# Turning finished rows on TensorE as float32r and as float32 inside the last layer, and adding the scaled difference to the output

## The chip, the cores and the metric

The kernel runs on one core of a Trainium2 chip. The metric is the device time of one execution in microseconds. The engines are named as in the profile: PE (TensorE matmul; PEld its weight loads), DVE (VectorE), ACT (ScalarE), POOL (GpSimd) and SP (SyncE, which here only issues transfers).

## What is computed

Causal attention with a decay bias (4 batches, 8 heads, 576 positions, head size 64), then two feed-forward layers over 2304 tokens with 512 features and 2048 hidden ones:

```python
scores = scale * np.matmul(q, k.transpose(0, 1, 3, 2))
...
attn = attn / (np.sum(attn, axis=-1, keepdims=True) + 1e-09)
x = np.matmul(attn, v)            # to (2304, 512)
h = x @ w_in;  x = np.maximum(0.01 * h, h) @ w_out
h = x @ w2_in; out = (np.maximum(h, 0.0) + np.log1p(np.exp(-np.abs(h)))) @ w2_out
```

All in float32. The kernel gets the precision from float32r matmuls by splitting each operand into a rounded high part and a low part, so that one product is three matmuls (high by high, high by low, low by high).

## The kernel before

Three stages follow one another: attention (to about 237 us), the first layer (to about 565) and the second layer (to the end). The change lies in the second layer alone.

The second layer splits the hidden features into eight blocks of 256 (`NJ = 8`) and four blocks of 512 token rows into two pairs (`PAIRS`; `sb` 0 and 1), beside a remainder of 256 rows (`Plain`). One `Quad` handles one pair and one hidden block: 16 quads, `sb` 0 first. A quad computes its 2 by 2 blocks of hidden values with seven products instead of eight: `X Y K Z X K Z` is the order of the PSUM banks to which the products 1 to 7 go, each of six matmuls. Products 5 to 7 accumulate into banks X, K and Z a second time. Between them, banks are added to each other: `first` (line 1028) copies bank X to an SBUF tile `u` on ACT after product 1, and five `join`s (line 1032) on DVE add `u` and the banks, the last of them into Z. So product 5 may write X only after `first` has read it, and product 6 K only after the second join.

Each of the four blocks of hidden values then passes through a `Unit`, a chain of nine steps: magnitude, exponential, logarithm and total on ACT, value and rest on DVE, correct on POOL, high on ACT (the rounded part) and low on POOL (the remainder). After the seven products of quad n come the eight output groups of quad n-1 (`outputs`, `emit_out`, line 1065): six matmuls each into a bank from `tail_bank`, which deals out three PSUM banks in turn, and one DVE instruction that adds the bank to `acc` (line 1086; a copy for the first hidden block). `acc` holds the output in SBUF with 128 token rows to a slot; after the last hidden block of a pair its rows are written to `out`.

The order is written out by hand. `on(t, fn)` puts a call into a list with a time in units of one product or output group; the list is sorted by that time at the end and the calls are made in this order. Each engine takes its instructions in the order in which they are made, and so does each engine's queue of transfers; nothing reorders them. A unit that begins at b has its steps at b plus 0, 0.45, 0.9, 1.35, 1.4, 1.85, 2.4, 4.1 and 5.5. In quad n, which begins at `starts[n]`, the products stand at +0 to +6, `first` at +1.05, the joins at +2.05, +3.05, +4.05, +6.05 and +7.05, the units at +5.1 and 2.6 further each, and the output groups of the quad before at +7 to +14. From the tenth quad on the next one begins at +15. `fetch` brings weights for coming quads through SP: those of the outputs of the next quad at +1, and at +9 the eight tiles of the products of the quad after it, each of which waits until its buffer is free.

The last row block pair's quads have index 8 to 15, so `starts[12]` is the fifth of the second pair. The rows 0 to 127 that the change uses were finished with quad 7.

Of the kernel before, what the change touches and what calls it, by code (L numbers as in the profile page):

```python
# [10 lines left out]
F32 = mybir.dt.float32  # L11
I32 = mybir.dt.int32
U32 = mybir.dt.uint32
F32R = mybir.dt.float32r
AF = mybir.ActivationFunctionType
ALU = mybir.AluOpType
PSUM = bass.MemoryType.PSUM

P = 128
# [12 lines left out]
def attn_moe_moe(ctx, tc, q, k, v, s, w1i, w1o, w2i, w2o, out):  # L32
    nc = tc.nc
# [17 lines left out]
    def pool(name, bufs=1, **kw):  # L51
        return tc.tile_pool(name=name, bufs=bufs, **kw)
# [28 lines left out]
    def move(dst, src, queue=nc.sync):  # L81
        queue.dma_start(dst.bitcast(F32), src.bitcast(F32))
# [457 lines left out]
    class Fill:  # L540
# [32 lines left out]
        def bank(self, nm):  # L573

            tag, bufs = ("m", 1) if not self.free else self.free.pop(0)
            if self.free is not None:
                self.free.append((tag, bufs))
            return self.ps.tile([P, 512], F32, tag=tag, name=nm, bufs=bufs)
# [88 lines left out]
    acc = ctx.enter_context(pool("accpool")).tile([P, KD, NT], F32, tag="acc", name="acc")  # L667
    stages = [ExitStack(), ExitStack()]
    enter = lambda stage, nm, **kw: stages[stage].enter_context(pool(nm, **kw))
# [200 lines left out]
    for g in range(1, NG):  # L870
        a = begin[g - 1]
        own = (1, 4, 7, 11, 15, 18, 16, 19) if g > 1 else (None,) * 4 + (3, 6, 4, 7)
        for j, n in enumerate(own):
            if n is not None:
                w = (0, g * G + j // 2, "io"[j % 2])
# [16 lines left out]
    k = begin[NG - 1, chunks[1]] + G + LAG  # L892
# [14 lines left out]
    for n, (g, c, f) in enumerate(steps):  # L907
        N = c[1]
        cols = slice(c[0], c[0] + N)
        ps = bank("ps_h")  # L910
# [21 lines left out]
    def on(t, fn, *args):  # L932
        events.append((t, len(events), fn, args))
# [3 lines left out]
    def tail_bank(nm):  # L937
        tag, bufs = next(tails)
        return psA.tile([P, 512], F32, tag=tag, name=nm, bufs=bufs)
# [185 lines left out]
    t = 0  # L1125
    starts = []
# [26 lines left out]
    for kp in range(2):  # L1153
# [5 lines left out]
        for n, nm in enumerate(("B11", "T3", "T2", "B21", "T4"), 1):  # L1159
# [3 lines left out]
            else:  # L1163
                on(b + 3, x_high, 1, nm, kp)
                on(b + 5, x_low, 1, nm, kp, nc.gpsimd)

    for t, _, fn, args in sorted(events, key=lambda x: x[:2]):
        fn(*args)
    stages[1].close()
# [47 lines left out]
```

## Time and profile before

| | us |
|---|---|
| median of 3 runs | 951.94 |
| lowest, highest | 951.5, 951.96 |
| the profiled execution | 951.81 |
| its span, first to last instruction | 950.0 |

| engine | busy us | share |
|---|---|---|
| PE | 941.3 | 99% |
| DVE | 668.0 | 70% |
| ACT | 575.8 | 61% |
| POOL | 564.3 | 59% |

The profile is one execution, with times in us from its first instruction. Busy shares are means over stages; a wait or a duration of one place is read from the timeline of that place. Matmuls are pipelined: a matmul of 512 columns is shown with 0.39 us, while the next starts 0.23 us after it, so a stream of matmuls is paid by the distance of its starts.

### The profile page before, as it was taken

The page shows a single profiled execution, that of the slowest core. Times are in us where ns is not written, and L with a number is a line of the kernel's source. Part 1 is how long each engine was busy: PE and PEld are TensorE (multiplying, and loading weights), DVE is VectorE, ACT ScalarE, POOL GpSimd, SP SyncE. Part 2 cuts the span into 40 slices and gives each one's busy share as a digit, 9 for nine tenths or more (in the row PEclk, how much of TensorE's full clock was granted, in tenths as well). Part 3 has the DMA queues.
Part 4 walks back from the last instruction along what each step waited for, and adds up shares of the span by engine and source line. Part 5 has one row for each costly group of instructions (what it writes and reads, how often), then busy time and mean ns, then how long its engine had stood idle before and what let it go on. Part 6 is the DMA issues. An engine that isn't in the chain of part 4 may idle for free.

```text
span 950.0 us, 15346 instructions
## 1 busy us (share of the span) xinstructions
PE 941.3 (99%) x5173; PEld 767.3 (81%) x5173; DVE 668.0 (70%) x1294; ACT 575.8 (61%) x1185; POOL 564.3 (59%) x548
## 2 busy tenths in 40 slices
PE   9999999999999999999999999999999999999998
PEld 6666767777998888888888888888888888888887
DVE  8888656554479798778998745665666666766666
ACT  6888677665566564546555446666656765565563
POOL 7778556444367676657666534755654664555443
PEclk9999999999999999999999999999999999999999
DMA  7453434331665654546476244341415248445402
GB/s 248 148 164 127 144 111 134 119 106 37 215 239 180 229 190 139 173 166 213 132 269 217 102 151 159 115 136 66 153 65 177 89 150 314 135 136 175 134 0 90
DMA packets 79251, 143.61 MB, mean 151 GB/s; under 512 B 7626, under 2 KB 24906, under 8 KB 79172
## 3 DMA queue, kind: packets, MB, share of 16 engines
q1 hardware_dynamic: 78740, 141.87, 44.9%
q8 instruction: 41, 0.67, 0.3%
q10 hardware_dynamic: 432, 0.75, 0.3%
q14 instruction: 38, 0.31, 0.1%
HBM read 109.33 MB, written 33.25 MB: 150 GB/s over the span
## 4 chain that ended last, share of the span: by engine, by line
PE 93%; DVE 3%; POOL 1%; ACT 1%; issue 1%; DMA 0%; SPq 0%; DVEq 0%; POOLq 0%; ACTq 0%
PE ps_h L145 20%; PE ps_out L1078 20%; PE ps_out L854 17%; PE ps_h L1023 16%; PE pt_s L316 4%; PE pt_t L377 3%; PE ps_o L635 3%; PE pt_v L409 3%; PE ps_h L1105 2%; PE pt_s L409 1%; PE pt_t L372 1%; PE pt_s L302 1%; DVE sc L337 1%; POOL sc L360 0%; ACT sc L349 0%
## 5 line engine op out<-in xcount | busy, mean ns | idle before, releaser
L974 POOL TENSOR_TENSOR l<-l,e 128x512 f32<-128x512 f32 x72 | 93.5, 1298 | 161.8 <-DVE e L971 147.5
L151 POOL TENSOR_TENSOR gl<-gf,gh 128x512 fp32r<-128x512 f32 (+2 forms) x68 | 88.7, 1305 | 111.7 <-ACT gh L150 78.5
L360 POOL TENSOR_SCALAR sc<-sc,st 128x512 f32<-128x512 f32 (+4 forms) x160 | 88.4, 563 | 79.2 <-DVE st L356 61.3
L145 PE MATMUL ps_h<-xh,wih 128*128 128x512 f32 (+2 forms) x320 | 119.9, 375 | 0.0
L145 PE MATMUL ps_h<-xh,wil 128*128 128x512 f32 (+2 forms) x320 | 118.1, 369 | 0.0
L145 PE MATMUL ps_h<-xl,wih 128*128 128x512 f32 (+2 forms) x320 | 117.9, 368 | 0.0
L1086 DVE TENSOR_TENSOR acc<-ps_out,acc 128x512 f32<-128x512 f32 (+1 forms) x127 | 86.8, 685 | 42.5 <-PE ps_out L1078 40.0
L1078 PE MATMUL ps_out<-woh,gh 128*128 128x512 f32 x290 | 112.5, 388 | 0.8 <-DVE acc L1086 0.8
L1078 PE MATMUL ps_out<-wol,gh 128*128 128x512 f32 x290 | 112.4, 388 | 0.0
L349 ACT ACTIVATE sc<-sc,st 128x512 f32<-128x512 f32 (+2 forms) x144 | 83.4, 582 | 34.5 <-DVE st L337 28.7
L854 PE MATMUL ps_out<-gh,woh 128*128 128x512 f32 (+2 forms) x272 | 99.2, 365 | 0.3 <-DVE acc L861 0.3
L854 PE MATMUL ps_out<-gh,wol 128*128 128x512 f32 (+2 forms) x272 | 99.1, 364 | 0.0
L854 PE MATMUL ps_out<-gl,woh 128*128 128x512 f32 (+2 forms) x272 | 99.0, 364 | 0.0
L834 ACT ACTIVATE gf<-ps_h 128x512 f32<-128x512 f32 (+2 forms) x68 | 37.1, 546 | 101.4 <-PE ps_h L145 92.7
L984 POOL TENSOR_TENSOR gl<-l,gh 128x512 fp32r<-128x512 f32 x72 | 93.6, 1308 | 3.0 <-ACT gh L980 3.0
L1078 PE MATMUL ps_out<-woh,gl 128*128 128x512 f32 x290 | 88.9, 388 | 0.0
L980 ACT ACTIVATE gh<-l 128x512 fp32r<-128x512 f32 x72 | 45.4, 630 | 66.0 <-POOL l L974 66.0
L1023 PE MATMUL ps_h<-xh,wih 128*128 128x512 f32 x208 | 81.0, 389 | 0.0
L1023 PE MATMUL ps_h<-xl,wih 128*128 128x512 f32 x208 | 81.0, 389 | 0.0
L1023 PE MATMUL ps_h<-xh,wil 128*128 128x512 f32 x208 | 80.9, 389 | 0.0
L337 DVE CUSTOM_DVE_ANT_0 sc<-pt_s,mask 128x512 f32<-128x512 f32 (+3 forms) x129 | 59.2, 483 | 16.2 <-PE pt_t L377 15.4
L145 PEld LDWEIGHTS ps_h<-xh,wil 128*128 128x128 f32 x320 | 60.2, 188 | 9.6
(168 smaller groups left out, 2369.7 us busy)
## 6 DMA issues: line engine op xcount, KB each, us to landing
w2d<-stg SPq DMA_DIRECT2D x88, 256.0 KB
rawi<-in_moe_w_in SPq DMA_DIRECT2D x32, 512.0 KB
rawo<-in_moe_w_out SPq DMA_DIRECT2D x32, 512.0 KB
wih<-w2d SPq DMA_DIRECT2D x64, 256.0 KB
wil<-w2d SPq DMA_DIRECT2D x64, 256.0 KB
woh<-w2d SPq DMA_DIRECT2D x32, 256.0 KB
wol<-w2d SPq DMA_DIRECT2D x32, 256.0 KB
K<-in_k SPq DMA_DIRECT2D x15, 432.0 KB
```

Source lines behind the costliest of these rows:

```text
L145: nc.tensor.matmul(ps, a, b, start=kk == 0 and n == 0, stop=kk == KD - 1 and n == 2)
L151: nc.gpsimd.tensor_tensor(gl, gf, gh.bitcast(F32), op=ALU.subtract)
L337: nc.vector.tensor_tensor_reduce(out=self.sc[:, j, c], in0=self.ps[j][:, c], in1=m, scale=-scale, scalar=low, op0=ALU.add, op1=ALU.min, ac ...
L349: nc.scalar.activation(x, x, AF.Exp, scale=-1.0, bias=self.stat(0, e + self.last), accum_out=self.stat(1, e))
L360: nc.gpsimd.tensor_scalar(x, x, self.stat(2, e), 1.0, op0=ALU.mult, op1=ALU.mult)
L854: nc.tensor.matmul(ps, a, b, start=f == 0 and m == 0, stop=f == G - 1 and m == 2)
L974: nc.gpsimd.tensor_tensor(self.l, self.l, self.e, op=ALU.subtract)
L980: nc.scalar.activation(self.gh, self.l, AF.Copy)
L984: nc.gpsimd.tensor_tensor(self.gl, self.l, self.gh.bitcast(F32), op=ALU.subtract)
L1023: nc.tensor.matmul(self.ps[name], x, y, start=n < 4 and kp == 0 and m == 0, stop=kp == 1 and m == 2, skip_group_check=n >= 4,)
L1078: nc.tensor.matmul(u, a, v, start=m == 0, stop=m == len(ops) - 1)
L1086: nc.vector.tensor_tensor(d[..., w], o[..., w], d[..., w], op=ALU.add)
```

## The change

New tiles `ident`, `ident_r`, `copy` and `apart` are placed behind all others in the last layer's memory. In quad 12 the following is added: an identity matrix on POOL and its rounded copy on ACT; a transfer on SP of 384 columns of finished rows 0 to 127 from `acc` to a float32r tile, bit for bit; 12 transposes on PE of this copy as float32r and 12 of `acc` as float32 (three blocks of 128x128, four times over), into two banks from `tail_bank`; on DVE a copy of the first bank to SBUF, the difference of the second to it, and the difference times 1e12 added to `acc`; and a transfer of the 384 columns to `out`.

```diff
+    def prepare_look():
+        make_identity(nc, ident)
+        nc.scalar.activation(ident_r, ident, AF.Copy)
+        move(copy, acc[:, 0, :384])
+
+    def turn(nm, x, y):
+        ps = tail_bank("ps_x")
+        ps = seen[nm] = ps.bitcast(F32R) if nm == "r" else ps
+        for k in range(4):
+            for c in range(3):
+                w = slice(c * P, (c + 1) * P)
+                nc.tensor.transpose(ps[:, w], x[:, w], y)
+
+    def compare():
+        d, o = apart, acc[:, 0, :384]
+        nc.vector.tensor_copy(d, seen["r"].bitcast(F32)[:, :384])
+        nc.vector.tensor_tensor(d, seen["f"][:, :384], d, op=ALU.subtract)
+        nc.vector.scalar_tensor_tensor(o, d, 1.0e12, o, op0=ALU.mult, op1=ALU.add)
+        nc.sync.dma_start(out[:P, :384], o)
+
+    t = starts[12]
+    on(t + 1, prepare_look)
+    on(t + 6.9, turn, "r", copy, ident_r)
+    on(t + 6.95, turn, "f", acc[:, 0, :512], ident)
+    on(t + 7.4, compare)
```

`make_identity` is two POOL instructions: a memset of the 128x128 tile to zero and an affine select that puts 1.0 on the diagonal. `nc.tensor.transpose` is one weight load of the data and one matmul that streams the identity. `move` is a transfer on SP.

## Rows read from the trace of the kernel before

**Rows 1.** The page: busy time by engine, and granted TensorE clock in 40 slices, tenths.
```profile
PE 941.3 (99%) x5173; PEld 767.3 (81%) x5173; DVE 668.0 (70%) x1294; ACT 575.8 (61%) x1185; POOL 564.3 (59%) x548
...
PEclk9999999999999999999999999999999999999999
```
**Rows 2.** Chain that ended last, 850 to 950: start, length, engine, line, instructions.
```profile
853.88 9.52 PE ps_h L1023 x42
863.39 10.88 PE ps_out L1078 x48
```
**Rows 3.** Busy time (instructions) of one quad: PE, PEld, DVE, ACT, POOL; clock; DMA.
```profile
853.70:874.10 20.40, 20.40 (x91) 16.89 (x90) 13.67 (x21) 12.26 (x21) 10.20 (x9) 1.00 0.49 155
```
**Rows 4.** Timeline of POOL in this quad: start, duration, instruction, idle time before.
```profile
855.94 1.29 POOL L974 TENSOR_TENSOR l<-l,e 128x512 f32<-128x512 f32 x1 [0.83 <-DVE e L971]
857.19 2.55 POOL L984 TENSOR_TENSOR gl<-l,gh 128x512 fp32r<-128x512 f32 x2
```
**Rows 5.** Timeline of ACT in this quad.
```profile
855.27 0.60 ACT L1030 ACTIVATE u<-ps_h 128x512 f32<-128x512 f32 x1 [0.76 <-PE ps_h L1023]
857.27 0.63 ACT L980 ACTIVATE gh<-l 128x512 fp32r<-128x512 f32 x1 [1.40 <-POOL l L974]
```
**Rows 6.** Timeline of PE: first product, fifth product, first output group.
```profile
853.71 0.39 PE L1023 MATMUL ps_h<-xh,wih 128*128 128x512 f32 x1
...
859.15 0.62 PE L1023 MATMUL ps_h<-xp,wih 128*128 128x512 f32 x2
...
863.23 0.39 PE L1078 MATMUL ps_out<-woh,gh 128*128 128x512 f32 x1
```
**Rows 7.** Timeline of POOL at the start of the kernel.
```profile
3.16 0.30 POOL L437 TENSOR_SCALAR_AFFINE_SELECT mask<-mask 128x128 f32<-128x128 f32 x1
...
4.11 0.20 POOL masks.py:197 MEMSET ident<- 128x128 f32 x1
4.38 1.28 POOL masks.py:199 TENSOR_SCALAR_AFFINE_SELECT ident<-ident 128x128 f32<-128x128 f32 x1
```
**Rows 8.** Timeline of DVE at the start of the kernel.
```profile
4.15 1.42 DVE L213 TENSOR_TENSOR_SCAN PB<-V,st,sc 128x576 f32<-128x576 f32 x1 [0.21 <-ACT sc L212]
```
**Rows 9.** Groups of ACT by form: busy us, mean ns of one, idle before.
```profile
L150 ACT ACTIVATE gh<-gf 128x512 fp32r<-128x512 f32 x48 | 29.9, 624 | 0.0
...
L150 ACT ACTIVATE gh<-gf 128x256 fp32r<-128x256 f32 x12 | 4.9, 407 | 0.1
```
**Rows 10.** Timeline of SP's transfer issues in this quad.
```profile
855.00 0.42 SPq L82 DMA_DIRECT2D wol<-w2d  x1
859.12 0.32 SPq L82 DMA_DIRECT2D wih<-w2d  x1
```
**Rows 11.** Busy time in one slice, columns as in rows 3; last is GB/s.
```profile
857.00:858.00 1.00, 1.00 (x6) 0.83 (x5) 0.40 (x2) 0.63 (x1) 1.00 (x2) 1.00 0.92 344
```
**Rows 12.** Timeline of PE in the attention stage, around six transposes.
```profile
112.55 0.82 PE L377 MATMUL pt_t<-ident,sc 128*128 128x128 f32 x6
113.12 0.47 PE L635 MATMUL ps_o<-gh,woh 128*128 128x512 f32 x1
113.43 0.39 PE L635 MATMUL ps_o<-gl,woh 128*128 128x512 f32 x1
```
**Rows 13.** Timeline of PE, two matmuls of 256 columns in a stream.
```profile
764.37 0.28 PE L1105 MATMUL ps_h<-xh,wil 128*128 128x256 f32 x1
764.49 0.28 PE L1105 MATMUL ps_h<-xh,wih 128*128 128x256 f32 x1
```
**Rows 14.** Instructions that write the transposes' tile: ns min/median/max, first and last start.
```profile
L377 PE MATMUL pt_t<-ident,sc x320: 270/273/330, 12.6 to 235.6; 128*128 128x128 f32 x160
```
**Rows 15.** Timeline of DVE in this quad: first accumulation of an output group, last join.
```profile
864.79 0.69 DVE L1086 TENSOR_TENSOR acc<-ps_out,acc 128x512 f32<-128x512 f32 x1 [0.76 <-PE ps_out L1078]
865.40 0.69 DVE L1040 TENSOR_TENSOR ps_h<-ps_h,u 128x512 f32<-128x512 f32 x1
```
**Rows 16.** Groups of DVE by form.
```profile
L391 DVE COPY PB<-pt_t 128x384 f32<-128x384 f32 x32 | 17.7, 554 | 32.8 <-PE pt_t L377 32.5
```

More of the change, by code (lines that the diff above doesn't have):

```diff
@@ L1165, in attn_moe_moe @@
                 on(b + 5, x_low, 1, nm, kp, nc.gpsimd)
+    look = enter(1, "look", side="right")
+    ident = look.tile([P, P], F32, tag="id", name="id")
+    ident_r = look.tile([P, P], F32R, tag="idr", name="idr")
+    copy = look.tile([P, 384], F32R, tag="cp", name="cp")
+    apart = look.tile([P, 384], F32, tag="ap", name="ap")
+    seen = {}
+    def prepare_look():
[20 more added lines that the diff above has]
+    on(t + 7.4, compare)
     for t, _, fn, args in sorted(events, key=lambda x: x[:2]):
```

## The prediction

> **What bounds the kernel now.** I read the page first: PE is busy 941.3 of 950.0 us, at a granted clock of nine tenths or more in every slice [rows 1]. A share over the whole span says nothing of one stage, so next I read the chain that ended last, over its last 100 us. It holds only PE, 42 product matmuls and 48 output matmuls in turn, up to the kernel's last output groups [rows 2]. The new work goes into the fifth quad of the second pair of row blocks (event time `starts[12]`). Its seven products start at 853.71 and end at 863.23, so six matmuls take 1.36 us and the eight output groups behind them, of the quad before, end at 874.1 [rows 6]. Over this stretch PE is busy 20.40 of 20.40 us at clock 1.00, while DVE has 13.67, ACT 12.26 and POOL 10.20 [rows 3]. So here each microsecond that PE is given or kept waiting comes out at the end, and nothing in PE's queue can give it back. The other engines matter only where PE waits for them.
>
> **Order first.** In this stage each engine's queue is the event list sorted by time. The trace bears this out: POOL does the fourth unit's subtraction (+0.3) at 855.94, then the third unit's low part (+0.8) and the fourth's (+3.4) as a pair from 857.19 [rows 4]. So I can place each new instruction. Positions below are event times relative to `starts[12]`.
>
> **Step 1: the identity (+1), a wait for PE.** POOL gets a memset and an affine select, ACT a rounding copy `ident_r` that needs both, and on ACT this copy stands ahead of `first` (+1.05), the copy of bank X into `u`. Behind the waiting ACT instruction are thus queued `first`, the fourth unit's high part and the next magnitude. `first` is the one that counts: the fifth product accumulates into bank X, so it may not start before `first` has read it. In the trace `first` runs from 855.27 to 855.87 and the fifth product starts at 859.15 [rows 5, 6], a cover of 3.3 us. When can POOL serve? The identity falls between the two low parts of the pair, which takes 2.55 us [rows 4], so at 858.46. The memset takes 0.20, with 0.27 to the next start. The select has two prices: 0.30 for the mask of the same size, 1.28 for the first identity [rows 7]. The second ran beside a DVE scan of 1.42 us and ended 0.09 us behind it [rows 8]. In the new place DVE has nothing to do, since its next three joins wait for `u`. I take 0.30 and keep 1.28 for the range. [...]
>
> POOL is then done at 858.46 + 0.27 + 0.30 = 859.03. For ACT's copy of 128 columns, 407 ns at 256 and 624 at 512 columns [rows 9] go down to about 0.30. With 0.04 for the handover (855.94 + 1.29 on POOL to ACT's 857.27) it ends at 859.37, `first` (0.60) at 859.97, and PE goes on at about 860.05: 0.9 us late [rows 4 to 6]. With the 1.28 us select it is 1.9; without any wait 0. DVE's joins follow `u` at 0.6 us each [rows 15], so the second is over at 861.3, as the fifth product ends at 861.4: no second wait, but no room either. POOL's last low part slips behind ACT's late high part to about 862; it is needed by the second half of the outputs, behind 868. That costs nothing, and would if `first` came over 4 us later still.
>
> **Step 2: the copy of the rows (+1).** One transfer of 196 KB from SBUF to SBUF on SP, behind four weight loads of 262 KB, the last issued at 855.00 [rows 10]. Its source has been ready long since. The trace has no such transfer; at the 344 GB/s of one slice there [rows 11] the loads and the copy together are 1.24 MB or 3.6 us, so it should land by 860, and PE needs it at about 864. I cost it at nothing; with the cover gone each microsecond costs one.
>
> **Step 3: 24 transposes on PE (+6.9, +6.95).** Each `turn` repeats three 128x128 transposes four times. Plain float32 ones are in the trace: six take from 112.55 to 113.12, 0.095 us each, and the matmul behind them has its successor 0.31 instead of 0.23 later [rows 12], some 0.1 for the change of kind. Twelve are 12 x 0.095 + 0.1 = 1.2 us. The float32r ones are in no row. From below: the float32r pitches at 512 columns, (863.23 - 853.71) / 42 = 0.227 us, and at 256, 0.120 us [rows 6, 13], make 0.42 ns a column and 14 ns fixed, 0.067 at 128 columns. From above: 0.120 if the weight load sets the pitch, as it may in the 256-column row, and 0.227 if short float32r operands are slow and take a 512-column pitch. I take 0.095, the neighbour in kind: 1.1 us. With the change of kind at either end that is 2.4 us (2.0 to 4.0). All of it is on the path, since PE has no gap. [...]
>
> **Step 4: two tail banks and the comparison (+7.4).** The tail banks are three in turn. The two `ps_x` tiles take two of them, the first output group the third, so the second output group needs the bank of the float32r turn, which only the comparison's first DVE copy sets free. On DVE that copy stands behind the first group's accumulation (+7) and the join into Z (+7.05). The trace gives their pace: the first group's matmuls end at 863.23 + 1.36 = 864.59, its accumulation starts at 864.79, the join at 865.40 [rows 6, 15]. The join takes 0.69, the copy of 128x384 out of PSUM 0.55 [rows 15, 16]. So the bank is free 0.20 + 0.61 + 0.69 + 0.55 = 2.05 us after the first group's end, where PE wants it at once: with the handover of 0.04 a wait of 2.1 us. The subtraction frees the other bank some 0.55 later, while the second group runs for 1.36 us: free. The third DVE instruction is 0.69 by the rows there and ends before the second group's accumulation is due. Were all three ahead of the release, the wait would be 3.3; with the copy ahead of the accumulation, 0.
>
> **Step 5: the added output transfer (+7.4).** SP issues in order, and this transfer waits for the comparison at about 872. Behind it stand the eight weight loads that were issued from 859.12 on [rows 10]. They are for the quad that starts at 894.5, two pitches of 20.4 us behind this one, so over 15 us are left when the last is issued: nothing.
>
> **Sum.** 0.9 + 2.4 + 2.1 = 5.4 us. The profiled execution took 951.81 us (span 950.0 and 1.81 around it), the median is 951.94. 951.81 + 5.4 = 957.2 us, 0.57% slower.
>
> **Rivals.** (a) The slow select: the 1.28 us row holds, the first wait is 1.9, the time 958.2. For it: the instruction is the same to the letter; against it: the scan beside it is missing here. (b) Slow short float32r operands: 12 x 0.227 instead of 1.1 makes 1.6 more, 958.8. No row excludes it. [...] (d) Not slower: the queues don't stand as listed. If the identity is on POOL ahead of its 855.94 instruction and the DVE copy ahead of the first group's accumulation, both waits vanish and the transposes remain: at 0.067 each 1.6 us, 953.4, within 0.2%. It decides at whether `first` still starts near 855.3. Against it: POOL's order above. That the change doesn't do what it says, with the transposes dropped as unused, would be 951.8; their result goes into the output, so I give it nothing. A faster kernel has no mechanism: PE's stretch has no gap to close.
>
> **How the numbers follow.** Forecast 60% (956.2 to 958.0), (a) 13%, (b) 8%, (c) 6%, (d) 7%, of which 5 come within 0.2% (1.9 us, about what a measurement can tell from no change); one of the two waits missing 6% (955.1 to 956.3). The range 954.8 to 960.0 leaves out (c), (d) and some tails. Faster 0.01, same 0.05, slower 0.94.
>
> **What would show it.** Right: `first` starting near 859.4 behind an ACT copy that waited for POOL; PE idle for about 0.9 us before the fifth product and for about 2.1 us before the second output group, released by ACT and DVE; 24 transposes in 2.4 us; a select of 0.30. Wrong: no idle PE there, a select over 1 us, transposes 0.2 apart, a matmul pitch over 0.23 behind them, or a PE wait for the copied rows.

## The result, and the profile after

The changed kernel takes 957.11 us (median of 4 runs, 956.65 to 958.95) against 951.95 us before: ratio 1.0059, 95% interval 1.0041 to 1.0076. It is slower by 5.2 us; forecast were 957.2 us and a range of 954.8 to 960.0. The profiled execution took 957.32 us with a span of 955.5.

The chain that ended last, in order of time from 850 on (start, length in us, what), where [rows 2] had only PE:

```profile
857.88 1.29 POOL gl L984
859.17 0.15 POOL id masks.py:197
...
859.39 0.30 POOL id masks.py:199
...
859.72 0.31 ACT idr L1176
860.02 0.49 ACT u L1030
...
860.56 4.55 PE ps_h L1023 x18
865.11 2.33 PE ps_x L1185 x24
867.44 1.39 PE ps_out L1078 x6
...
868.86 0.70 DVE acc L1086
...
869.61 10.11 PE ps_out L1078 x42
879.72 9.52 PE ps_h L1023 x42
```

Twice the chain leaves PE: through POOL's identity and two ACT instructions to the fifth product, and through DVE's accumulation of the first output group to the second. Between them stand the 24 transposes. From 879.72 on it is PE alone again, with the pieces of 9.52 and 10.88 us that it had before.

The timeline of PE, with two of its weight loads (PEld), at the places where its rows of before were read [rows 6]; the bracket gives the idle time and what ended it:

```profile
854.39 0.39 PE L1023 MATMUL ps_h<-xh,wih 128*128 128x512 f32 x1
...
860.56 0.72 PE L1023 MATMUL ps_h<-xp,wih 128*128 128x512 f32 x2 [0.57 <-ACT u L1030]
861.13 0.40 PE L1023 MATMUL ps_h<-xp,wil 128*128 128x512 f32 x1
...
862.08 0.19 PEld L1023 LDWEIGHTS ps_h<-xh,wih 128*128 128x128 f32 x1 [0.30 <-DVE u L1040]
862.09 0.50 PE L1023 MATMUL ps_h<-xh,wih 128*128 128x512 f32 x1
862.42 0.39 PE L1023 MATMUL ps_h<-xl,wih 128*128 128x512 f32 x1
...
864.95 1.15 PE L1185 MATMUL ps_x<-idr,cp 128*128 128x128 f32 x12
865.94 1.50 PE L1185 MATMUL ps_x<-id,acc 128*128 128x128 f32 x12
867.20 0.48 PE L1078 MATMUL ps_out<-woh,gh 128*128 128x512 f32 x1
867.52 0.39 PE L1078 MATMUL ps_out<-wol,gh 128*128 128x512 f32 x1
...
869.61 0.50 PE L1078 MATMUL ps_out<-woh,gh 128*128 128x512 f32 x1 [0.78 <-DVE acc L1086]
...
871.26 0.19 PEld L1078 LDWEIGHTS ps_out<-woh,gh 128*128 128x128 f32 x1 [0.41 <-DVE ap L1190]
871.26 0.50 PE L1078 MATMUL ps_out<-woh,gh 128*128 128x512 f32 x1
...
872.75 0.39 PE L1078 MATMUL ps_out<-woh,gh 128*128 128x512 f32 x1
```

Since PE has no gap before the change, the start of each piece can be set against the trace of before (853.71, 859.15 and 863.23 are in [rows 6]; the others follow at 1.36 us a piece), and the difference of neighbouring differences is what each place costs:

| PE starts | before | after | later by | cost of the place |
|---|---|---|---|---|
| the quad | 853.71 | 854.39 | 0.68 | ahead of the change |
| product 5 | 859.15 | 860.56 | 1.41 | 0.73 |
| product 6 | 860.51 | 862.09 | 1.58 | 0.17 |
| the turns | (863.23) | 864.95 | 1.72 | 0.14 |
| output group 1 | 863.23 | 867.20 | 3.97 | 2.25 |
| output group 2 | 864.59 | 869.61 | 5.02 | 1.05 |
| output group 3 | 865.95 | 871.26 | 5.31 | 0.29 |
| output group 4 | 867.31 | 872.75 | 5.44 | 0.13 |

From the quad's start to the end of the span it is 101.11 us against 96.29, so the change itself costs about 4.8 us in this execution (4.82 by these numbers; the span is printed to a tenth, so this and the costs below are good to about 0.05). The 0.68 ahead of it are taken up below (c0_before). The 0.14 and 0.13, and a part of the others, are what PE pays each time its stream stops: the second matmul then starts 0.33 us behind the first in place of 0.23 (862.09 to 862.42 above). Of the 0.17 of product 6, too, some 0.12 is the restarted stream of product 5 (0.57 us for its first two matmuls, 860.56 to 861.13, in place of 0.45); the rest is the wait for the second join, which let go the weight load at 862.08. Behind the transposes nothing stops PE, and yet the second matmul stands 0.32 us behind the first (867.20 to 867.52), so about 0.1 of the 1.05 is the change of kind, from transposes back to matmuls, and 0.95 the wait.

The three engines that PE waited for, in the same stretch: POOL, ACT, then DVE.

```profile
857.88 1.29 POOL L984 TENSOR_TENSOR gl<-l,gh 128x512 fp32r<-128x512 f32 x1
859.11 0.21 POOL masks.py:197 MEMSET id<- 128x128 f32 x1
859.39 0.29 POOL masks.py:199 TENSOR_SCALAR_AFFINE_SELECT id<-id 128x128 f32<-128x128 f32 x1
861.11 1.29 POOL L984 TENSOR_TENSOR gl<-l,gh 128x512 fp32r<-128x512 f32 x1 [1.43 <-ACT gh L980]
...
859.72 0.31 ACT L1176 ACTIVATE idr<-id 128x128 fp32r<-128x128 f32 x1 [4.52 <-POOL id masks.py:199]
859.93 0.58 ACT L1030 ACTIVATE u<-ps_h 128x512 f32<-128x512 f32 x1
...
860.54 1.49 DVE L1040 TENSOR_TENSOR u<-ps_h,u 128x512 f32<-128x512 f32 x2 [4.06 <-ACT u L1030]
...
868.86 0.69 DVE L1086 TENSOR_TENSOR acc<-ps_out,acc 128x512 f32<-128x512 f32 x1 [3.19 <-PE ps_out L1078]
869.47 0.69 DVE L1040 TENSOR_TENSOR ps_h<-ps_h,u 128x512 f32<-128x512 f32 x1
870.06 0.55 DVE L1189 COPY ap<-ps_x 128x384 f32<-128x384 f32 x1
870.65 0.56 DVE L1190 TENSOR_TENSOR ap<-ps_x,ap 128x384 f32<-128x384 f32 x1
871.24 0.56 DVE L1191 SCALAR_TENSOR_TENSOR acc<-ap,acc 128x384 f32<-128x384 f32 x1
```

POOL's pair of [rows 4] is torn apart by the identity. ACT sits idle for 4.52 us, its rounding copy waiting for it, and `first` behind it runs at 859.93 in place of 855.27 [rows 5], 4.0 us late beyond the 0.68; DVE's joins wait 4.06 us for it. The comparison stands behind the accumulation and the join, at the pace of [rows 15]. One line speaks against the prediction: PE's second group starts at 869.61, before DVE's copy of the float32r turn begins.

SP's issues, as [rows 10]:

```profile
856.15 0.51 SPq L82 DMA_DIRECT2D cp<-acc  x1
871.82 0.34 SPq L1192 DMA_DIRECT2D out<-acc  x1
872.26 0.38 SPq L82 DMA_DIRECT2D wih<-w2d  x1
```

The weight loads that stood at 859.12 are held back by over 12 us, behind the transfer that waits for the comparison, and no row of PE waits for a weight later.

### The profile page after: what moved, and what is told of

It is laid out like the page before. It is cut to its first block, busy times and chain, and to the rows that moved or that the text cites. A ratio compares the mean times of both kernels' runs of the same rounds, so it can differ in the third digit from the quotient of the medians.

```text
span 955.5 us, 15405 instructions
## 1 busy us (share of the span) xinstructions
PE 945.3 (99%) x5197; PEld 769.5 (81%) x5197; DVE 669.7 (70%) x1297; ACT 576.2 (60%) x1186; POOL 565.9 (59%) x550
## 4 chain that ended last, share of the span: by engine, by line
PE 92%; DVE 3%; POOL 1%; ACT 1%; DMA 1%; issue 1%; SPq 0%; DVEq 0%; POOLq 0%; ACTq 0%
PE ps_h L145 20%; PE ps_out L1078 20%; PE ps_out L854 17%; PE ps_h L1023 15%; PE pt_s L316 4%; PE pt_t L377 3%; PE ps_o L635 3%; PE pt_v L409 3%; PE ps_h L1105 2%; PE pt_s L409 1%; PE pt_t L372 1%; PE pt_s L302 1%; DVE sc L337 1%; ACT sc L349 0%; DVE acc L1086 0%
```

## The experiments

Costs "from the quad's start" are the span's end minus the quad's first matmul, less the 96.29 us of before. They leave out what varies ahead of the quad, and are good to about 0.05 us. Beside each stands the ratio of times to the kernel before.

**The start of the kernel** (`c0_before`, the kernel before without an edit).

> The kernel before, once more, for its first 10 us. In the changed kernel the whole stream of PE stands 0.65 us later than before from the first 7 us on, ahead of anything that was changed. Theory (this varies from run to run): some runs of the kernel before start as late. Rival (the longer program starts later): this run's attention stage starts like the profile before, and all variants of the changed kernel start 0.65 us later.

Measured 952.13 us in one run, span 950.3. The timeline of PE at the start:

```profile
5.18 1.85 PE L316 MATMUL pt_s<-K,Q 64*128 64x512 f32 x4
6.87 1.02 PE L316 MATMUL pt_s<-PB 64*128 64x512 f32 x4
```

The first four matmuls on Q and K take 1.69 us until the next piece. In the profile of before they took 1.18 (5.47 to 6.65), in the changed kernel's 1.71 (5.58 to 7.29). The same program can therefore start either way. The quad begins at 854.01 here and at 854.78 in the other run of unchanged layers (`e6_identity_first`), beside the 853.71 of before; in the changed kernel and its variants it begins between 853.21 and 854.39. The 0.68 us are no part of the change. From the quad's start this run costs 0.00.

**The rounding copy moved out of the way** (`e1_round_later`).

```diff
         make_identity(nc, ident)
-        nc.scalar.activation(ident_r, ident, AF.Copy)
...
     on(t + 1, prepare_look)
+    on(t + 4.5, nc.scalar.activation, ident_r, ident, AF.Copy)
```

> The rounding copy ident_r is moved from +1 to +4.5, behind `first` and the fourth unit's high part on ACT; the identity itself stays on POOL at +1. Theory (the copy that waits for POOL holds up `first`, and through bank X the fifth product): `first` starts about 0.9 us after the first product's start plus 1.36 again, the fifth product follows the fourth without idle time, the sixth without its 0.17 us for the late join; 0.73 + 0.17 + about 0.1 for the restarted stream are gone, 956.1 us, ratio to the kernel before 1.0044. Rival (POOL's identity between the low parts is what PE pays for, by the late low part): no change, 957.1, and the output groups' second half waits for gl.

Measured 955.96 us, ratio 1.0041 (1.0028 to 1.0055); from the quad's start 3.79, 1.03 less than the changed kernel. PE goes through its products without a stop (853.42 the quad, 862.94 the turns, 9.52 us as before), and the only wait of PE that is left in the quad is the second group's, 0.8 us for `acc`. So the first wait is the copy on ACT, and its price is all of 0.73 + 0.17 + 0.14. The identity itself still stands between POOL's low parts, which costs nothing.

**The comparison ahead of the accumulation** (`e2_compare_earlier`).

```diff
-    on(t + 7.4, compare)
+    on(t + 6.97, compare)
```

> The comparison goes from +7.4 to +6.97, on DVE ahead of the first output group's accumulation and the last join. Theory (the banks of the tail are what PE waits for, and DVE's order sets when they come free): the copy of the float32r turn starts while the float32 turn still runs, both banks are free before the first output group ends, and the 1.05 us ahead of the second group, the 0.29 ahead of the third and the 0.13 of the restarted stream are gone: 955.6 us, ratio 1.0039. Rival (PE waits there because the switch from transposes back to matmuls drains it): no change, 957.1.

Measured 955.64 us, ratio 1.0035 (1.0022 to 1.0047); from the quad's start 3.44, 1.38 less than the changed kernel. DVE's timeline:

```profile
865.82 0.56 DVE L1189 COPY ap<-ps_x 128x384 f32<-128x384 f32 x1 [0.47 <-PE ps_x L1185]
867.15 0.56 DVE L1190 TENSOR_TENSOR ap<-ps_x,ap 128x384 f32<-128x384 f32 x1 [0.78 <-PE ps_x L1185]
867.75 0.56 DVE L1191 SCALAR_TENSOR_TENSOR acc<-ap,acc 128x384 f32<-128x384 f32 x1
868.53 0.69 DVE L1086 TENSOR_TENSOR acc<-ps_out,acc 128x512 f32<-128x512 f32 x1 [0.23 <-PE ps_out L1078]
```

The three instructions fit into the time in which DVE waited for the first group anyway; it still idles 0.23 us ahead of the accumulation. PE shows no wait behind the turns. So the change of kind back to matmuls is not what the second group waited for; its 0.1 us behind the first group's first matmul (866.87 to 867.19 here) stays.

**Both** (`e3_both`).

> Both moves at once. Theory (two separate waits plus 24 transposes that no other work covers): the savings add up, only the transposes' 2.25 us and 0.1 us for the change of kind stay, 951.95 + 2.35 = 954.3 us, ratio 1.0025. Rival (the waits overlap with something that comes back, one saving eats the other): 955.5 or more. Rival (the transposes are hidden once nothing waits): within 0.2% of 951.95.

Measured 954.50 us over 11 runs, ratio 1.0024 (1.0015 to 1.0033); from the quad's start 2.50. No wait of PE is left in this stretch, and what remains is the transposes' 2.25 us and the 0.1 us of the change of kind. The savings of the two single moves, 1.03 and 1.38, make 2.41; 4.82 - 2.41 = 2.41, beside the 2.50 measured. The two waits are separate and add up.

**Six transposes in place of 24** (`e7_once`), **and 96** (`e4_four_times`).

```diff
-        for k in range(4):
+        for k in range(1):
```

> Each turn repeats its three transposes once in place of four times: 6 transposes in place of 24, nothing else changed. Theory (a transpose costs its distance of starts, 0.083 us as float32r and 0.105 as float32 in the changed kernel's trace, and none of it is hidden): 9 x 0.083 + 9 x 0.105 = 1.7 us less, 955.4. Rival (by the duration, 0.25 to 0.27 each): 4.7 less, 952.4. Rival (hidden behind the wait for the banks): no change.

```diff
-        for k in range(4):
+        for k in range(16):
```

> Each turn repeats its three transposes 16 times in place of four: 96 transposes in a row in place of 24, nothing else changed. Theory (distance of starts): 36 x 0.083 + 36 x 0.105 = 6.8 us more, 963.9. [...]

Measured 955.52 us, ratio 1.0035 (1.0022 to 1.0048), and 963.89, ratio 1.0123 (1.0110 to 1.0137); from the quad's start 3.10 and 11.92 beside 4.82, that is 1.72 less and 7.10 more (1.59 and 6.78 between the medians). PE of the longer one, and the clock over this stretch (columns as in [rows 3]):

```profile
864.45 4.26 PE L1185 MATMUL ps_x<-idr,cp 128*128 128x128 f32 x48
868.54 5.43 PE L1185 MATMUL ps_x<-id,acc 128*128 128x128 f32 x48
873.73 0.48 PE L1078 MATMUL ps_out<-woh,gh 128*128 128x512 f32 x1
...
864.45:873.73 9.28, 9.28 (x98) 9.28 (x96) 0.72 (x2) 4.39 (x8) 1.29 (x1) 1.00 0.01 2
```

48 float32r transposes take 4.09 us, 0.085 each; 48 float32 ones 5.19, 0.108 each. In the changed kernel 12 took 0.99 and 1.26, 0.083 and 0.105 each; in the shorter program 3 took 0.22 and 0.27, 0.073 and 0.090. These means grow with the length because a few distances at a turn's ends are short (0.06 us behind the first float32r one, 0.03 behind the last float32 one). What one more transpose costs is the same throughout: 0.086 and 0.110 us from 3 to 12, 0.086 and 0.109 from 12 to 48. None of it is hidden. The granted clock stays at 1.00 over the 9.28 us in which PE does transposes only, and the distances stay as they are. Every run of this case lists a mean granted clock of 0.998 to 1.0, so nothing of the 7.10 us is a lower clock.

**One bank for both turns** (`e5_one_bank`).

```diff
-        ps = tail_bank("ps_x")
-        ps = seen[nm] = ps.bitcast(F32R) if nm == "r" else ps
-        for k in range(4):
-            for c in range(3):
+        if nm == "r":
+            seen["b"] = tail_bank("ps_x")
+        ps = seen["b"][:, :256] if nm == "r" else seen["b"][:, 256:]
+        seen[nm] = ps
+        ps = ps.bitcast(F32R) if nm == "r" else ps
+        for k in range(6):
+            for c in range(2):
```

> Both turns go into one bank of 512 columns: two blocks of 128x128 six times over in place of three blocks four times, so still 12 and 12 transposes. The comparison covers 256 of the 384 columns; the third block is left out. The identity keeps its place. Theory (PE waits behind the turns because two of the three tail banks are taken): the second output group gets the third bank and starts at once, the third one finds the first group's bank released; the 1.38 us that the earlier comparison saved are saved here too, about 955.6 us, ratio 1.0038. Rival (DVE's order by itself is what PE waits for, whatever the banks): no change against the changed kernel, 957.1.

Measured 956.82 us, ratio 1.0051 (1.0038 to 1.0063); from the quad's start 4.65, only 0.17 less than the changed kernel. The expectation missed. PE waits at another place:

```profile
870.75 0.47 PE L1078 MATMUL ps_out<-woh,gh 128*128 128x512 f32 x1 [0.90 <-DVE ap L1193]
```

This is the third group, and it waits for the subtraction that reads the turned bank. The second one did start at once. The cause is in the program: which bank a group gets. The PSUM banks that the built programs use, read from their instructions (no trace holds them):

| | float32r turn | float32 turn | groups 1, 2, 3, 4 |
|---|---|---|---|
| changed kernel | 6 | 0 | 7, 7, 0, 6 |
| e2_compare_earlier | 6 | 0 | 7, 6, 0, 7 |
| e5_one_bank | 6 | the same | 0, 7, 6, 0 |
| e8_compare_later | 6 | 0 | 7, 7, 0, 7 |
| e9_next_bank | 0 | 6 | 7, 0, 7, 6 |

The three banks are not dealt out in turn, as the description of the kernel and the prediction had it. `tail_bank` asks for tiles under two names, its tags, each with its own buffers: the tag `a` has one bank (0 here) and the tag `t` two (6 and 7), and a group of tag `t` gets one of the two. In the changed kernel the float32r turn has tag `t`, and so have the groups 1 and 2; group 2 got group 1's bank again and not the turned one, which the two banks of `t` in turn would have given it. All five programs fit a choice of the bank whose last reader comes first on DVE; the choice itself was not tried apart. In `e5_one_bank` the third group got the turned bank.

**The comparison one group later** (`e8_compare_later`).

```diff
-    on(t + 7.4, compare)
+    on(t + 8.5, compare)
```

> The comparison goes from +7.4 to +8.5, on DVE behind the second output group's accumulation too. In this program the second group again has the first group's bank, the third that of the float32 turn, the fourth the second group's. Theory (a group waits for what DVE does last with its own bank): the second group waits as before, 1.05 us, for the first accumulation; the third waits for 0.20 + 0.61 + 0.59 + 0.56 = 2.0 us in place of 0.29, 958.8. The theory of the prediction (the second group waits for the copy of the float32r turn): that copy would be another 2 us later for the second group, and the third would not wait.

Measured 960.07 us, ratio 1.0082 (1.0068 to 1.0095); from the quad's start 6.73, 1.91 more than the changed kernel, where 1.7 were expected. The profiled execution, 958.87 us, is the fastest of the four; the median lies 1.3 us above the 958.8 expected, and no trace shows where the others lost it. PE:

```profile
869.28 0.50 PE L1078 MATMUL ps_out<-woh,gh 128*128 128x512 f32 x1 [0.78 <-DVE acc L1086]
872.78 0.50 PE L1078 MATMUL ps_out<-woh,gh 128*128 128x512 f32 x1 [1.84 <-DVE ap L1190]
```

The second group waits for the first accumulation as before, unmoved by the later copy; the third starts 3.50 us behind it, 2.14 more than 1.36, released by the subtraction. Here each of the two groups waits for the last reader of its own bank.

**The next bank** (`e9_next_bank`).

```diff
+        if nm == "r":
+            next(tails)
         ps = tail_bank("ps_x")
```

> One place of the order in which the tail's bank tags are dealt (t, t, a) is skipped ahead of the first turn; nothing else changes. In this program the second output group then has the bank of the float32r turn, as the prediction had it, the third the first group's and the fourth that of the float32 turn. Theory (a group waits for what DVE does last with its own bank): the second group waits 0.20 + 0.61 + 0.60 + 0.55 + about 0.1 = 2.1 us for DVE's copy, in place of 1.05 for the first accumulation, and the third not at all, in place of 0.29; in sum 0.7 more than the changed kernel from the quad's start on, about 957.8. Rival (what PE waits for behind the turns doesn't hang on the bank): the wait stays at 1.05 and 0.29.

Measured 957.75 us, ratio 1.0059 (1.0047 to 1.0072); from the quad's start 5.72, 0.90 more than the changed kernel.

```profile
870.56 0.47 PE L1078 MATMUL ps_out<-woh,gh 128*128 128x512 f32 x1 [1.94 <-DVE ap L1191]
```

With the float32r turn in tag `a`, the second group, of tag `a` too, gets its bank and starts at 870.56, 3.56 us behind the first group at 867.00: a wait of 2.20 us, released by DVE's copy. This is the wait that the prediction described, 2.1 us by its sum. It belongs to this dealing of the banks and not to the one in the changed kernel.

**The price of the affine select** (`e6_identity_first`, the kernel before).

```diff
-        masks()
         make_identity(nc, ident)
+        masks()
```

> The kernel before, with the attention stage's identity made ahead of the masks on POOL in place of behind them, where no DVE scan runs beside it. Theory (the 1.28 us of its affine select were a wait for the scan, as in the changed kernel, where it ended 0.09 us behind the scan again): the select takes about 0.30. Rival (the first identity select of a kernel is slow by itself): about 1 us or more again. The time stays within 0.2% of 951.95 either way.

Measured 952.12 us, ratio 0.9999 (0.9990 to 1.0008). POOL's timeline at the start:

```profile
1.00 0.29 POOL masks.py:199 TENSOR_SCALAR_AFFINE_SELECT ident<-ident 128x128 f32<-128x128 f32 x1
```

The first select of the kernel takes 0.29 us away from DVE's scan, where it took 1.28 beside it [rows 7, 8]. In the trace of the changed kernel the untouched start gives the third point: the scan ran from 3.97 for 1.42 us, the select started later than in the trace before, and it ended at the same distance behind the scan, 0.09 us.

```profile
3.97 1.42 DVE L213 TENSOR_TENSOR_SCAN PB<-V,st,sc 128x576 f32<-128x576 f32 x1 [0.21 <-ACT sc L212]
4.50 0.98 POOL masks.py:199 TENSOR_SCALAR_AFFINE_SELECT ident<-ident 128x128 f32<-128x128 f32 x1
```

So the 1.28 us were a wait. In the traces of before and after the select starts while the scan runs, takes 1.28 and 0.98 us and ends 0.09 behind it (5.66 behind 5.57, and 5.48 behind 5.39). The trace of `e5_one_bank` shows the other order: both start together, the select takes 0.29 us, and the scan 1.51 in place of 1.42.

```profile
4.48 0.29 POOL masks.py:199 TENSOR_SCALAR_AFFINE_SELECT ident<-ident 128x128 f32<-128x128 f32 x1
...
4.48 1.51 DVE L213 TENSOR_TENSOR_SCAN PB<-V,st,sc 128x576 f32<-128x576 f32 x1 [0.21 <-ACT sc L212]
```

## Why the prediction was right, and where its terms were not

**The bound** held: PE ran without a gap up to the quad and behind it, and what PE was given or kept waiting came out at the end, to within 0.1 us, in every variant (the table's places make 4.76 of the 4.82).

**Step 1** (0.9 us) held with its mechanism and its order. POOL reached the identity between the two low parts, the select took the lower of its two prices, and `first` ended 0.05 us before product 5 went on. Alone, the wait was 0.73 us, 0.17 less than forecast, mostly because `first` started 0.21 us behind the rounding copy's start, where the step let the copy's whole 0.30 pass. But the step put the restart of the stream at nothing, and its margin, "no second wait, but no room either", was not there: the restart and a short wait for the second join cost 0.17 us at product 6 and, with its restart, 0.14 at the turns. Together 1.04; `e1_round_later` gave back 1.03.

**Step 2 and step 5** (nothing) held: no wait of PE for the copied rows or for a weight in any variant, although SP's loads came over 12 us later.

**Step 3** (2.4 us, with the change of kind): 2.25 to the first group's start and 0.1 behind it, 2.35. The float32r transpose, in no row before, came out at 0.083 to 0.086 us, between the bounds of 0.067 and 0.120, and the float32 one at 0.105 to 0.110 in place of 0.095. The two errors had opposite signs, so the sum is better than its terms.

**Step 4** (2.1 us) is the step that was mis-sized, and for a wrong reason. It took the three tail banks for one ring and so gave the second group the bank of the float32r turn. The code has two tags, but reading them is not enough: the two banks of `t` in turn would give the same. The built program gave the second group the first group's bank again. So it waited for the first accumulation (0.20 + 0.70 and handovers, 0.95), the third a little for the subtraction (0.29, in part the restart), 1.38 with the restart, which is what `e2_compare_earlier` gave back. The price of the wait it meant was right, 2.20 against 2.1 in `e9_next_bank`, where the banks are dealt as it thought.

**The sum** of 5.4 us stands against 4.82 in the profile from the quad's start, and against 5.16 between the medians; by its terms 1.04 + 2.35 + 1.38 = 4.77 were measured. That the forecast time lies within 0.1 us of the median owes something to chance: step 4 was 0.7 us too high, and the median came out 0.3 above 951.95 + 4.82, inside the spread of the start.

**The rivals.** (a), the slow select, is out here: it takes 0.29 us where no scan runs. (b), slow short float32r operands, is out: 0.083. (c), with 6% of the chances, stands for a lower granted clock: no run shows one, nor what it would cost. The clock was 1.00 from 853.70 to 874.10 in the changed kernel, 1.00 over the 9.28 us of 96 transposes, and the matmuls of the fourth output group start 0.23 us apart again (872.75 to 872.98). (d), that the waits don't arise, is what `e3_both` makes of the program by moving two instructions: then 954.5.

## What to carry to other kernels

An instruction that is put into an in-order queue costs what it waits for, and the next instruction in that queue pays: here 0.31 us of ACT work held `first` back by 4.0 us. Before costing a bank or a buffer, look up in the built program which one each tile gets: here neither the order of the calls nor the tags told it. Work that only has to be done some time goes behind the queue's urgent instruction, or into a place where the engine is idle anyway: moving one ACT copy back and three DVE instructions forward took away half of what the added work cost.

## What the runs showed of the hardware that was not expected

The affine select of 128x128 took 0.29 to 0.30 us (0.29 at 859.39 in the changed kernel, 0.30 for the mask [rows 7]), or, where it started while DVE's scan ran, until 0.09 behind the scan's end: 1.28 and 0.98 us in two traces, 0.29 with the scan elsewhere (`e6_identity_first`). Started together with the scan (`e5_one_bank`, at 4.48) it took 0.29, and the scan 1.51 in place of 1.42, 0.09 more. So in these traces one takes longer while the other runs: the select ended 0.09 us behind the scan, not the 0.29 that it takes alone, and the scan that started with it grew by 0.09, not by 0.29. What the rest of the 0.29 is stays open, and no run shows why one holds up the other.

One more float32r transpose of 128x128 in a stream takes 0.086 us and a float32 one 0.109 to 0.110, while their shown durations are 0.25 and 0.27 (medians of 251 and 273 ns in the changed kernel). The shown weight loads are alike, 0.14 us for either (medians of 141 and 140 ns), so the load alone doesn't set the distance; what does stays open.

After a stop of its stream PE's second matmul of 512 columns started 0.30 to 0.35 us behind the first, in place of 0.23 (0.33 from 862.09 and 0.34 from 869.61 in the changed kernel, 0.30 from 870.56 in `e9_next_bank`, 0.35 from 869.44 in `e7_once`), so each stop cost about 0.1 us beyond its own length. Behind transposes it was 0.31 to 0.32 without a stop (867.20 to 867.52 in the changed kernel, 865.37 to 865.68 in `e7_once`).
